# Linear attention between feed-forward products: the two heads' scores taken in turn, and the products on the tensor engine put into fewer groups

## The chip, the cores and the metric

The kernel runs on one core of a Trainium2 chip. The metric is the time of one execution on the device in microseconds. Engines are named as in the profile: PE is TensorE (matrix products), PEld its weight loads, DVE is VectorE, ACT is ScalarE, POOL is GpSimd and SP is SyncE, which issues DMAs.

## The reference

A gated linear attention over 768 steps, for 4 batches of 8 heads of width 48, is followed by two feed-forward blocks on the 384 channels of each batch.

```
f = 1.0 / (1.0 + np.exp(-f_logit))
for t in range(S):                       # S = 768, B = 4, H = 8, D = 48
    state = f[:, :, t, :, None] * state + np.einsum('bhd,bhe->bhde', k[:, :, t], v[:, :, t])
    y[:, :, t] = np.einsum('bhd,bhde->bhe', q[:, :, t], state)
# x: (B, S, 384) from y
h = gelu(x @ w_in)                       # 384 -> 1024; u, v its halves
v_n = normalised(v) * g_ln
v_s = np.einsum('ts,bsd->btd', w_sg, v_n) + b_sg[None, :, None]
x = x + (u * v_s) @ w_out
theta = x @ w_theta
y = np.einsum('ts,bsd->btd', w_tok_r, x * cos(theta)) + np.einsum('ts,bsd->btd', w_tok_i, x * sin(theta))
u = x + y
out = u + np.maximum(u @ w_ch, 0.0)
```

## The kernel before, in words

**Attention.** The sequence is cut into blocks of 128 steps. Within a block the decays are multiplied up, so that the recurrence becomes products of matrices. A *unit* (function `unit`, from L547) treats two heads (j = 0, 1) over half a sequence (hf = 0, 1), that is three blocks c of 128 steps. There are 4 batches x 2 halves x 4 pairs of heads, 32 units. Head 0 lies in partitions 0 to 47 of the tile `qkv` (in batch 0's second half of tiles named `ar`), head 1 in 64 to 111. A unit's work on PE before the change is:

- three transposes of the keys into one bank of PSUM (L567), which ACT copies to `kt` (L571);
- the scores of head 0, three products, and then, as an operation of its own, those of head 1 (L580); each has a bank, and DVE multiplies each by the causal mask into a tile `am` (L585);
- the updates of the state (L596), two for each block, with the last block left out where hf is 1; DVE and ACT make from them the chain of states `s` (L609, L619);
- three operations of outputs, one for each block: two masked products, `am` with the values (L631), and, where there is a state before the block, two state products (L635), which add to the same columns. ACT copies the bank to `y` (L639), and POOL sends it to `xst` by DMA (L647).

The products are of float32, and each stands in the trace as two instructions. So the scores of a unit are twelve instructions at L580, the masked products twelve at L631, the updates twelve or eight at L596, the state products eight (hf 0) or twelve (hf 1) at L635.

**Feed-forward blocks.** `mm3` (L666 to L668) makes one product of two split operands by three matrix products of 384 or 512 columns. Their weights are decoded by DVE and ACT (L413 to L434) from wide floats while the products run.

**Order.** The class `Plan` writes out the order of every engine's instructions ahead of time. Each operation is given a duration, on PE a number of columns too, and a virtual time at which it is wanted. A list schedule takes, at each step, the operation that can start first and, among those, the one wanted first. Buffers of a kind (`Slots`) are taken in the order in which they were asked for; attention has four banks of PSUM, `at`, and in the first half of batch 0 those of the feed-forward blocks, `mm`, too. Attention of batch 1 is spread over the first feed-forward block of batch 0, and that of batches 2 and 3 over later work. Up to a planned time of 100 us, gaps on PE are filled with products of no use (`idle`, L908), written into bank `at0` beside the columns in use. On the chip each engine follows its order and waits at semaphores.

Of the kernel before, what the change touches and what calls it, by code (L numbers as in the profile page):

```python
# [17 lines left out]
P = 128  # L18
# [70 lines left out]
class Buf:  # L89
    """A tile (or a part of one) whose readers and writers order each other."""  # L90
# [9 lines left out]
class Part:  # L100
    """A part of a tile, by its first free index."""
# [13 lines left out]
class Plan:  # L115
    """Orders the instructions of each engine: a list schedule over their estimated times."""
# [47 lines left out]
    @staticmethod  # L164
    def loads(o, table):
        """the activation tables that the operation has to load ("T": tanh, which two of them have)"""
        if o.table is None or o.table == table or (o.table == "T" and table in ("G", "S")):
            return None
        return "G" if o.table == "T" else o.table

    def schedule(self):
# [14 lines left out]
        def slot_time(o):  # L186
            t = 0.0
            for b in o.need:
                if b.held:
                    continue  # L190
                s = b.slots
                if s.order[s.next] is not b:
                    return None
                best = None
                for i in range(s.n):
                    prev = s.owner[i]
                    if prev is None:
                        u = 0.0
                    else:
                        u = 0.0  # L200
                        for a in prev.acc:
                            if a.end is None:
                                u = None
                                break
                            u = max(u, a.end + (0.0 if a.dma else lat(a.eng, o.eng)))
                    if u is not None and (best is None or u < best[0]):
                        best = (u, i)
                if best is None:
                    return None
                b.slot = best[1]  # L210
                t = max(t, best[0])
            return t

        def run(a, dur, left):
            """the tensor engine's clock: up after a tick with enough columns"""
            c, i = left / dur, int(a / TICK + 1e-9)
            while left > 1e-6:
                rate = c if ticks.get(i - 1, 0) >= 3060 else c / 2
                n = min(left, rate * ((i + 1) * TICK - a))
                ticks[i] = ticks.get(i, 0) + n  # L220
                left, a, i = left - n, a + n / rate, i + 1
            return a
# [89 lines left out]
def body(tc, ctx, att, qkv, flog, w_in, g_ln, w_sgT, b_sg, w_out, w_theta, w_rT, w_iT, w_ch, out):  # L312
# [67 lines left out]
    # ------------------------------------------------------------------ pieces  # L380
# [12 lines left out]
    def load_f32(pl, g, dst, src, on_act, vt, after=(), background=False):  # L393
        """dst: a function that gives the float32 tile; src: float32, or the bits of float64"""
# [31 lines left out]
    def load_split(pl, g, hi, lo, his, src, vt, scale=None, on_act=False, after=(), background=False):  # L426
        """hi, lo: buffers; his: a function that gives their tiles"""
        n = src.shape[-1]
        t = pl.buf(g.w32 if background else g.dt, [P, TH])
        load_f32(pl, g, (t, lambda: t.t[:, :n]), src, on_act, vt, after, background)  # L430
        if scale is not None:
            pl.op("ACT", a1(n), lambda: nc.scalar.mul(t.t[:, :n], t.t[:, :n], scale), [], [t], vt=vt)
        pl.op("ACT", a1(n), lambda: nc.scalar.copy(his()[0], t.t[:, :n]), [t], [], hi, vt=vt)  # L433
        pl.op("DVE", v1(n), lambda: nc.vector.tensor_sub(his()[1], t.t[:, :n], his()[0].bitcast(F32)), [t, *hi], [], lo, vt=vt)  # L434
# [47 lines left out]
    # --------------------------------------------------------------- attention  # L482
    def attention(pl, g, b, v0, v1_):
        """the gated linear attention of batch b, spread over the virtual times v0..v1_"""
# [10 lines left out]
    def half(pl, g, b, hf, xst, carry, vt, step):  # L495
# [3 lines left out]
        if b == 0 and hf == 1:  # L499
            # the feed-forward block's tiles are still free  # L500
# [23 lines left out]
        for p0, p1 in groups:  # L524
# [13 lines left out]
            # within a block the decays multiply up; at its first step the second operand starts it anew  # L538
# [8 lines left out]
    def unit(pl, g, b, hf, p, f, fb, seed, sb, be, bb, t, parts, xst, carry):  # L547
# [8 lines left out]
        # ks = -k / b: one Newton step on the seed of 1 / b  # L556
# [15 lines left out]
        ams = []  # L572
        for j in range(2):
            aps = bank(1 + j)
            am = pl.buf(g.am, [P, NC2, P])
            r = slice(64 * j, 64 * j + D)

            def scores(aps=aps, r=r):
                for c in cs:
                    nc.tensor.matmul(aps.t[:, c], K()[r, c], Q()[r, c], start=True, stop=True)  # L580

            pl.op("PE", 0.64, scores, r=[kb, qb], w=[aps], cols=576)
            pl.op(
                "DVE", v1(TH),
                lambda aps=aps, am=am: V.tensor_tensor(am.t, aps.t[:, :TH].rearrange("p (c t) -> p c t", c=NC2), mask3, ALU.mult),  # L585
                r=[aps], w=[am],
            )
            ams.append(am)
        ups = bank(3)
        nu = NC2 - hf  # the last block's state isn't needed  # L590

        def updates():
# [8 lines left out]
        pl.op("PE", 0.1 * nu, updates, r=[kt, vb], w=[ups], cols=192 * nu)  # L601
        state = carry.pop(p) if hf else None
# [23 lines left out]
        yps = bank(4)  # L626
        for c in range(NC2):

            def outputs(c=c, s=states[c]):
                for j in range(2):  # L630
                    nc.tensor.matmul(yps.t[HP * j : HP * j + HP, cs[c]], VT(c, j, HP), ams[j].t[:, c], start=True, stop=s is None)  # L631
                if s is not None:
                    for j in range(2):
                        r = slice(HP * j, HP * j + D)
                        nc.tensor.matmul(yps.t[r, cs[c]], s.t[r], Q()[r, cs[c]], start=False, stop=True)  # L635

            pl.op("PE", 0.45, outputs, r=[vb, qb, *ams] + ([states[c]] if states[c] else []), w=[yps], cols=540 if states[c] else 270)
# [14 lines left out]
    # ---------------------------------------------------------------------- MoE  # L652
    def moe(pl, g, xst, get, wmid, out_b, pace, first=False):
        """the two blocks of a batch; their before(): what the last block left over, to run in the first gap"""
# [3 lines left out]
        def mm3(ps, a, bs, start, stop, n):  # L658
            """one product of two split operands; a, bs: ((hi buffer, lo buffer), tiles)"""
# [241 lines left out]
    # -------------------------------------------------------------------- order  # L901
# [3 lines left out]
    def idle(n):  # L905
        """products of no use, which keep the tensor engine's clock up until those of use come"""
        for _ in range(n):
            nc.tensor.matmul(g.at.tiles[0][:, TH:], ident, ident, start=True, stop=True)  # L908

    pl.idle = idle  # L910
    with tc.manual_schedule():
# [20 lines left out]
        # the second blocks of the first two batches come late: their weights are decoded meanwhile  # L932
# [24 lines left out]
    # decays that float32's range doesn't carry through a block: the recurrence step by step  # L957
# [141 lines left out]
```

## Time and profile before

| what | value |
|---|---|
| median of 3 timed runs | 691.79 us |
| lowest and highest | 690.66 and 695.57 us |
| span of the profiled execution (its own time; nothing is recorded around it) | 697.4 us |
| PE, DVE, ACT busy | 97%, 69%, 61% of the span |

The span is that of one profiled execution, from its first instruction to its last. PE's busy time counts each instruction from its start to its modelled end, so instructions that overlap are shown together as one row with a count in the timeline. [...]

### The profile page before, as it was taken

How to read it: one execution, taken by the hardware profiler on the slowest of the kernel's cores; microseconds unless marked ns; L12 is line 12 of the kernel's file. 1: busy time of each engine (PE TensorE's matmuls, PEld its weight loads, DVE VectorE, ACT ScalarE, POOL GpSimd, SP SyncE). 2: the span in 40 equal slices, each digit the busy share in tenths (PEclk: the TensorE clock that was granted, in tenths of full speed). 3: DMA queues.
4: the chain of work that ended last, by engine and by line, in shares of the span. 5: the costliest groups of instructions: out<-in, count | busy, mean ns of one | idle time of the engine just before them, and what ended most of it. 6: DMA issues, size and time to landing. Idle time of an engine off the chain costs nothing.

```text
span 697.4 us, 12027 instructions
## 1 busy us (share of the span) xinstructions
PE 678.8 (97%) x4353; PEld 595.2 (85%) x4353; DVE 483.0 (69%) x1040; ACT 428.7 (61%) x905; POOL 93.7 (13%) x163
## 2 busy tenths in 40 slices
PE   7998999999999999999999999999999999998996
PEld 7765677977889989998898788889888889998995
DVE  5769986986999988755965666657754454567533
ACT  6568987955886678544973469535753455347520
POOL 2221233133131010003201211110010000000000
PEclk9556699999999999999999999999999999999999
DMA  8734356558356623348344551322143341111422
GB/s 324 264 105 137 107 176 203 190 171 284 126 159 189 220 66 135 124 123 260 109 143 147 155 175 41 98 63 75 32 155 102 94 153 35 35 50 35 162 74 73
DMA packets 42613, 93.55 MB, mean 134 GB/s; under 512 B 6064, under 2 KB 28208, under 8 KB 41520
## 3 DMA queue, kind: packets, MB, share of 16 engines
q1 hardware_dynamic: 33840, 63.00, 28.3%
q0 software_dynamic: 8704, 29.70, 13.0%
q8 instruction: 36, 0.59, 0.4%
q14 instruction: 33, 0.27, 0.1%
HBM read 76.15 MB, written 11.80 MB: 126 GB/s over the span
## 4 chain that ended last, share of the span: by engine, by line
PE 84%; DVE 6%; ACT 3%; DMA 2%; issue 2%; POOL 1%; SPq 0%; DVEq 0%; ACTq 0%; POOLq 0%
PE mm L666 22%; PE mm L668 20%; PE mm L667 20%; PE at L580 6%; PE at L631 4%; PE at L635 4%; PE at L596 2%; PE at L567 2%; PE mm L762 1%; DMA raw<-in_w_iT 1%; PE mm L580 1%; DMA f<-in_flog 1%; DMA dt<-in_w_sgT 1%; PE at L908 1%; DVE tmp L726 1%
## 5 line engine op out<-in xcount | busy, mean ns | idle before, releaser
L666 PE MATMUL mm<-st,ar 128*128 128x384 f32 x480 | 166.6, 347 | 1.9 <-ACT u L708 1.4
L667 PE MATMUL mm<-st,ar 128*128 128x384 f32 x480 | 161.3, 336 | 0.4 <-DVE st L434 0.4
L668 PE MATMUL mm<-st,ar 128*128 128x384 f32 x480 | 161.1, 336 | 0.0
L434 DVE TENSOR_TENSOR st<-dt,st 128x384 fp32r<-128x384 f32 x144 | 77.7, 553 | 72.3 <-ACT st L433 71.8
L433 ACT CAST st<-dt 128x384 fp32r<-128x384 f32 x144 | 72.7, 511 | 87.1 <-PE mm L668 54.6
L666 PEld LDWEIGHTS mm<-st,ar 128*128 128x128 f32 x480 | 90.4, 188 | 9.5 <-issue 5.1
L667 PEld LDWEIGHTS mm<-st,ar 128*128 128x128 f32 x480 | 90.5, 189 | 0.9 <-DVE st L434 0.9
L668 PEld LDWEIGHTS mm<-st,ar 128*128 128x128 f32 x480 | 90.4, 188 | 0.0
L685 ACT CAST x<-xst 128x384 fp32r<-128x384 f32 x72 | 36.1, 510 | 42.0 <-DVE xst L690 24.5
L647 POOL DMA_DIRECT2D xst<-y x80 | 40.5, 511 | 141.6 <-ACT y L639 91.5
L585 DVE TENSOR_TENSOR am<-at,mask 128x384 f32<-128x384 f32 x60 | 31.6, 550 | 22.2 <-PE at L580 14.1
L675 ACT CAST ar<-tmp 128x384 fp32r<-128x384 f32 x80 | 38.0, 511 | 8.2 <-DVE tmp L731 7.3
L686 DVE TENSOR_TENSOR x<-xst,x 128x384 fp32r<-128x384 f32 x72 | 38.6, 552 | 5.7 <-ACT x L685 5.4
L676 DVE TENSOR_TENSOR ar<-tmp,ar 128x384 fp32r<-128x384 f32 x80 | 41.0, 550 | 2.2 <-ACT ar L675 1.8
L690 DVE TENSOR_TENSOR xst<-xst,mm 128x384 f32<-128x384 f32 x48 | 26.0, 552 | 21.8 <-PE mm L668 21.6
L580 PE MATMUL at<-qkv 48*128 48x128 f32 x312 | 40.4, 298 | 0.0
L580 PEld LDWEIGHTS at<-qkv 48*128 48x128 f32 x312 | 33.4, 195 | 6.8 <-issue 5.6
L666 PE MATMUL mm<-ar,wout 128*128 128x384 f32 x96 | 33.9, 353 | 1.6 <-DVE tmp L778 1.6
L631 PE MATMUL at<-am,qkv 128*64 128x128 f32 x312 | 34.9, 306 | 0.0
L666 PE MATMUL mm<-x,win 128*128 128x384 f32 x96 | 33.9, 353 | 0.0
L518 POOL DMA_DIRECT2D qkv<-in_qkv x24 | 13.3, 554 | 147.6 <-PE at L635 132.7
L667 PE MATMUL mm<-ar,wout 128*128 128x384 f32 x96 | 32.9, 343 | 0.0
(156 smaller groups left out, 1478.9 us busy)
## 6 DMA issues: line engine op xcount, KB each, us to landing
dt<-scratch SPq DMA_DIRECT2D x96, 192.0 KB, 2.4
qkv<-in_qkv POOLq DMA_DIRECT2D x24, 536.0 KB, 4.7
dt<-in_w_sgT SPq DMA_DIRECT2D x48, 192.0 KB, 2.7
wmid<-scratch SPq DMA_DIRECT2D x6, 1152.0 KB, 5.8
raw<-in_w_rT SPq DMA_DIRECT2D x12, 384.0 KB, 4.1
raw<-in_w_iT SPq DMA_DIRECT2D x12, 384.0 KB, 3.3
f<-in_flog POOLq DMA_DIRECT2D x6, 768.0 KB, 4.9
scratch<-wt POOLq DMA_DIRECT2D x24, 192.0 KB, 3.1
```

The lines of the kernel that those rows point to most:

```text
L433: pl.op("ACT", a1(n), lambda: nc.scalar.copy(his()[0], t.t[:, :n]), [t], [], hi, vt=vt)
L434: pl.op("DVE", v1(n), lambda: nc.vector.tensor_sub(his()[1], t.t[:, :n], his()[0].bitcast(F32)), [t, *hi], [], lo, vt=vt)
L580: nc.tensor.matmul(aps.t[:, c], K()[r, c], Q()[r, c], start=True, stop=True)
L631: nc.tensor.matmul(yps.t[HP * j : HP * j + HP, cs[c]], VT(c, j, HP), ams[j].t[:, c], start=True, stop=s is None)
L647: lambda r0=r0, n=n, kc=kc, o=64 * j + off: q[YQ].dma_start(xst.t[r0 : r0 + n, kc], y.t[o : o + n]),
L666: nc.tensor.matmul(o, h0, h1, start=start, stop=False)
L667: nc.tensor.matmul(o, h0, l1, start=False, stop=False)
L668: nc.tensor.matmul(o, l0, h1, start=False, stop=stop)
L675: pl.op("ACT", a1(n), lambda: nc.scalar.copy(tiles()[0], src.t[:, :n]), [src], [hi])
L676: pl.op("DVE", v1(n), lambda: V.tensor_sub(tiles()[1], src.t[:, :n], tiles()[0].bitcast(F32)), [src, hi], [lo])
L685: pl.op("ACT", a1(TH), lambda: nc.scalar.copy(X[hf][:, 0, k], T()), [src], [hi])
L686: pl.op("DVE", v1(TH), lambda: V.tensor_sub(X[hf][:, 1, k], T(), X[hf][:, 0, k].bitcast(F32)), [src, hi], [lo])
```

## The change

- The scores of the two heads become one operation. Its instructions go block by block, head 0 and head 1 in turn. It takes two banks at once.
- The updates and all masked products of a unit become one operation, `products`. It waits for `kt` and both `am` tiles, and takes the banks of the updates and of the outputs at once.
- The state products of a unit become one operation, `carried`, which waits for all states it needs.
- In the bank of the outputs, each head's sum is opened by its first masked product (`start` only at c = 0) and stays open until its last state product.
- The planner learns to give one operation two buffers of a kind (`slot_time`). The products of no use go to a bank without an open sum (`started`).
- The durations and columns that the planner is told change with it.
- Comments are removed.

```diff
         def slot_time(o):
-            t = 0.0
+            t, taken = 0.0, {}
             for b in o.need:
...
-                if s.order[s.next] is not b:
+                mine = taken.setdefault(id(s), [])
+                at = s.next + len(mine)
+                if at >= len(s.order) or s.order[at] is not b:
                     return None
...
                 b.slot = best[1]
+                mine.append(best[1])
...
-        ams = []
+        aps = [bank(1 + j) for j in range(2)]
+        ams = [pl.buf(g.am, [P, NC2, P]) for _ in range(2)]
+        rows = [slice(HP * j, HP * j + D) for j in range(2)]
+
+        def scores():
+            for c in cs:
+                for j in range(2):
+                    nc.tensor.matmul(aps[j].t[:, c], K()[rows[j], c], Q()[rows[j], c], start=True, stop=True)
+
+        pl.op("PE", 0.85, scores, r=[kb, qb], w=aps, cols=1152)
         for j in range(2):
-            aps = bank(1 + j)
-            am = pl.buf(g.am, [P, NC2, P])
-            r = slice(64 * j, 64 * j + D)
-
-            def scores(aps=aps, r=r):
-                for c in cs:
-                    nc.tensor.matmul(aps.t[:, c], K()[r, c], Q()[r, c], start=True, stop=True)
-
-            pl.op("PE", 0.64, scores, r=[kb, qb], w=[aps], cols=576)
...
-        ups = bank(3)
-        nu = NC2 - hf  # the last block's state isn't needed
-
-        def updates():
+        ups, yps = bank(3), bank(4)
+        nu = NC2 - hf
+        state = carry.pop(p) if hf else None
+
+        def products():
+            started.append(yps.t)
             for c in range(nu):
                 for j in range(2):
...
-        pl.op("PE", 0.1 * nu, updates, r=[kt, vb], w=[ups], cols=192 * nu)
-        state = carry.pop(p) if hf else None
+            for c in range(NC2):
+                for j in range(2):
+                    nc.tensor.matmul(yps.t[HP * j : HP * j + HP, cs[c]], VT(c, j, HP), ams[j].t[:, c], start=c == 0, stop=False)
+
+        pl.op("PE", 0.12 * nu + 0.87, products, r=[kt, vb, *ams], w=[ups, yps], cols=192 * nu + 810)
...
-        yps = bank(4)
-        for c in range(NC2):
-
-            def outputs(c=c, s=states[c]):
+        late = [c for c in range(NC2) if states[c] is not None]
+
+        def carried():
+            started.pop(next(i for i, t in enumerate(started) if t is yps.t))
+            for c in late:
                 for j in range(2):
-                    nc.tensor.matmul(yps.t[HP * j : HP * j + HP, cs[c]], VT(c, j, HP), ams[j].t[:, c], start=True, stop=s is None)
-                if s is not None:
-                    for j in range(2):
-                        r = slice(HP * j, HP * j + D)
-                        nc.tensor.matmul(yps.t[r, cs[c]], s.t[r], Q()[r, cs[c]], start=False, stop=True)
-
-            pl.op("PE", 0.45, outputs, r=[vb, qb, *ams] + ([states[c]] if states[c] else []), w=[yps], cols=540 if states[c] else 270)
+                    nc.tensor.matmul(yps.t[rows[j], cs[c]], states[c].t[rows[j]], Q()[rows[j], cs[c]], start=False, stop=c == late[-1])
+
+        pl.op("PE", 0.22 * len(late) + 0.2, carried, r=[qb, *(states[c] for c in late)], w=[yps], cols=270 * len(late))
...
         for _ in range(n):
-            nc.tensor.matmul(g.at.tiles[0][:, TH:], ident, ident, start=True, stop=True)
+            t = next(t for t in g.at.tiles if not any(t is x for x in started))
+            nc.tensor.matmul(t[:, TH:], ident, ident, start=True, stop=True)
```

## Rows read from the trace of the kernel before

**Rows 1.** The page: busy time of each engine; the group of the masks on DVE.

```profile
PE 678.8 (97%) x4353; PEld 595.2 (85%) x4353; DVE 483.0 (69%) x1040; ACT 428.7 (61%) x905; POOL 93.7 (13%) x163
...
L585 DVE TENSOR_TENSOR am<-at,mask 128x384 f32<-128x384 f32 x60 | 31.6, 550 | 22.2 <-PE at L580 14.1
```

**Rows 2.** Busy us by stretch: window, length, engines (x instructions), clock, DMA.

```profile
20.00:52.00 32.00, 32.00 (x194) 22.04 (x191) 21.08 (x49) 18.65 (x46) 7.51 (x13) 0.50 0.50 167
52.00:82.50 30.50, 27.94 (x184) 17.73 (x182) 28.82 (x74) 27.23 (x60) 7.13 (x14) 0.65 0.39 116
82.50:169.20 86.70, 85.60 (x625) 66.43 (x623) 71.76 (x167) 64.14 (x144) 26.07 (x44) 0.98 0.63 203
169.20:244.20 75.00, 73.50 (x402) 70.31 (x403) 69.26 (x149) 58.62 (x124) 12.65 (x17) 1.00 0.54 174
244.20:553.40 309.20, 308.77 (x2086) 272.45 (x2084) 203.39 (x423) 181.44 (x373) 33.80 (x59) 1.00 0.37 117
```

**Rows 3.** Waits of PE, 82.5 to 553.4 us: total, times, longest; the two largest.

```profile
PE mm L666 <- ACT u L708: 1.4, 1, 1.4
PE at L635 <- ACT s L619: 1.1, 2, 0.7
```

**Rows 4.** Timeline of PE, a spread unit of hf 0: start, duration, line, tiles, count.

```profile
464.50 1.26 PE L580 MATMUL at<-qkv 48*128 48x128 f32 x12
465.69 0.45 PE L666 MATMUL mm<-st,ar 128*128 128x384 f32 x1
...
466.94 0.56 PE L596 MATMUL at<-qkv,kt 128*64 128x48 f32 x12
467.42 0.45 PE L666 MATMUL mm<-st,ar 128*128 128x384 f32 x1
467.71 0.34 PE L667 MATMUL mm<-st,ar 128*128 128x384 f32 x1
467.88 0.34 PE L668 MATMUL mm<-st,ar 128*128 128x384 f32 x1
468.15 0.44 PE L631 MATMUL at<-am,qkv 128*64 128x128 f32 x4
468.52 0.45 PE L666 MATMUL mm<-st,ar 128*128 128x384 f32 x1
```

**Rows 5.** Timeline of PE, two blocks' masked products in a row.

```profile
453.24 0.66 PE L631 MATMUL at<-am,qkv 128*64 128x128 f32 x8
453.82 0.42 PE L635 MATMUL at<-qkv,s 48*48 48x128 f32 x4
454.18 0.44 PE L666 MATMUL mm<-x,win 128*128 128x384 f32 x1
```

**Rows 6.** Timeline of PE, one head's scores alone.

```profile
429.19 0.93 PE L580 MATMUL at<-qkv 48*128 48x128 f32 x6
430.06 0.44 PE L666 MATMUL mm<-st,ar 128*128 128x384 f32 x1
```

**Rows 7.** Timeline of PE, the last unit.

```profile
547.55 0.44 PE L596 MATMUL at<-qkv,kt 128*64 128x48 f32 x8
547.82 0.40 PE L631 MATMUL at<-am,qkv 128*64 128x128 f32 x4
548.15 0.42 PE L635 MATMUL at<-qkv,s 48*48 48x128 f32 x4
...
552.76 0.44 PE L631 MATMUL at<-am,qkv 128*64 128x128 f32 x4
```

**Rows 8.** Timeline of PE, updates followed by masked products.

```profile
89.99 0.56 PE L596 MATMUL at<-qkv,kt 128*64 128x48 f32 x12
90.38 0.40 PE L631 MATMUL at<-am,qkv 128*64 128x128 f32 x4
```

**Rows 9.** Timeline of PE in batch 0's first half, at the lower clock.

```profile
24.27 1.65 PE L580 MATMUL mm<-qkv 48*128 48x128 f32 x6
25.85 0.69 PE L631 MATMUL at<-am,qkv 128*64 128x128 f32 x4
26.47 0.67 PE L635 MATMUL at<-qkv,s 48*48 48x128 f32 x4
```

More of the change, by code (lines that the diff above doesn't have):

```diff
@@ L195, in slot_time @@
                 for i in range(s.n):
+                    if i in mine:
+                        continue
                     prev = s.owner[i]
[L197 to L200, printed above, removed]
+                    u = 0.0
+                    if prev is not None:
                         for a in prev.acc:
@@ L480, in stream @@
         return w
+    started = []
     def attention(pl, g, b, v0, v1_):
@@ L571, in unit @@
         pl.op("ACT", a1(TH), lambda: nc.scalar.mul(kt.t, kps.t[:, :TH], -1.0), r=[kps], w=[kt])
-        ams = []
-        for j in range(2):
-            aps = bank(1 + j)
-            am = pl.buf(g.am, [P, NC2, P])
-            r = slice(64 * j, 64 * j + D)
-            def scores(aps=aps, r=r):
-                for c in cs:
-                    nc.tensor.matmul(aps.t[:, c], K()[r, c], Q()[r, c], start=True, stop=True)
-            pl.op("PE", 0.64, scores, r=[kb, qb], w=[aps], cols=576)
+        aps = [bank(1 + j) for j in range(2)]
[6 more added lines that the diff above has]
+        pl.op("PE", 0.85, scores, r=[kb, qb], w=aps, cols=1152)
+        for j in range(2):
             pl.op(
                 "DVE", v1(TH),
-                lambda aps=aps, am=am: V.tensor_tensor(am.t, aps.t[:, :TH].rearrange("p (c t) -> p c t", c=NC2), mask3, ALU.mult),
-                r=[aps], w=[am],
-            )
-            ams.append(am)
-        ups = bank(3)
+                lambda j=j: V.tensor_tensor(ams[j].t, aps[j].t[:, :TH].rearrange("p (c t) -> p c t", c=NC2), mask3, ALU.mult),
+                r=[aps[j]], w=[ams[j]],
+            )
+        ups, yps = bank(3), bank(4)
         nu = NC2 - hf
-        def updates():
+        state = carry.pop(p) if hf else None
+        def products():
+            started.append(yps.t)
             for c in range(nu):
```

## The prediction

> **What bounds the kernel now.** I read the page's busy shares first: TensorE (PE) is busy for 97% of the span, VectorE (DVE) for 69%, ScalarE less [rows 1]. PE's share counts pipelined ends, so it had to be confirmed by stage. [...] The waits of PE from 82.5 to 553.4 confirm it: the two longest are 1.4 and 1.1 us in 471 [rows 3]. So from 82.5 us on a microsecond of PE's instruction stream is a microsecond of the end, as long as no other engine is full. Two stretches have another one nearly full: DVE is at 28.8 of 30.5 us (94%) from 52 to 82.5 and at 69.3 of 75.0 us (92%) from 169.2 to 244.2, and it is at 83% between them [rows 2]. The last attention work on PE is at 553 us; what follows is not touched.
>
> PE's stream I read from the timeline, by starts: a block costs the time from its start to the start of the next row. Durations overlap and would count double.
>
> **What the change does to PE's stream, in units.** A unit is one pair of heads over half a sequence; there are 32: 8 of batch 0, before 82.5 us, and 24 after it. In a unit that is spread among the feed-forward products [rows 4] the scores of both heads take 1.19 us (464.50 to 465.69), the updates 0.48, a block of masked products alone 0.37. Between two such blocks three feed-forward products take 0.73 us, with steps of 0.29, 0.17 and 0.27: the middle one is the undisturbed step, so each excursion to attention costs 0.73 - 3 x 0.174 = 0.2 us beyond its own block. A block of state products takes 0.36 (453.82 to 454.18) [rows 5]. Eight masked products in a row take 0.58 (453.24 to 453.82) where four take 0.37 [rows 4, 5], so two further pairs cost 0.21, that is 0.107 a pair: the two heads of a pair run side by side there, because the code alternates them.
>
> *Scores.* Six instructions, one head, take 0.87 us with the way in and out [rows 6]; the twelve of two heads take 1.19 [rows 4]. The second head overlaps already, but late: it adds 0.32. Alternated from the first instruction it should add about nothing, as for the masked products. So a unit's scores go from 1.19 to 0.87, and where the planner had parted the two heads, from 2 x 0.87 to 0.87. The bounds are a second head that adds nothing (0.87) and one that runs serially: six further steps of (1.19 - 0.87)/3 = 0.11 us, so 1.53. I take the first, by the masked products.
>
> [...]
>
> *Updates and masked products.* In the trace an update block that runs straight into masked products takes 0.39 (twelve instructions) or 0.27 (eight), and the four masked products behind it 0.33 instead of 0.37 [rows 7, 8]: these two kinds follow each other without a gap. The new group has twelve masked products, so 0.33 + 4 x 0.107 = 0.76; with the updates 1.15 in a first half (hf 0) and 1.03 in a second (hf 1).
>
> *State products.* They come in one block: 0.36 + 2 x 0.107 = 0.57 (two blocks of the sequence, hf 0) and 0.36 + 4 x 0.107 = 0.79 (three, hf 1). No row shows more than four of them in a row; if each further pair cost as much as half of a block of two (0.18), these would be 0.72 and 1.08. I take 0.107, by the masked products, which are as wide.
>
> *Sum for a spread unit.* A pair of blocks, masked and state products, is 0.37 + 0.36 = 0.73. hf 0 before: 1.19 + 0.48 + 0.37 + 2 x 0.73 + four excursions beside the one with the transposes, 0.8, makes 4.29; after: 0.87 + 1.15 + 0.57 + 0.4 = 2.99; it saves 1.30. hf 1 before: 1.19 + 0.37 (eight updates alone: 0.27 and the 0.1 by which twelve alone exceed 0.39) + 3 x 0.73 + 0.8 = 4.55; after: 0.87 + 1.03 + 0.79 + 0.4 = 3.09; it saves 1.46. With 12 of each: 33.1 us. Not every unit is spread: the timeline from 82.5 to 553.4 has 72 entries into such blocks (the first at 89.99, the last at 552.76 [rows 7, 8]) where 96 would be full spread, so 24 x 0.2 = 4.8 us less is to be won; and in 7 units the heads' scores are parted, as in [rows 6], which adds 7 x (1.74 - 1.19) = 3.9. That leaves 32.2 us, **1.34 us a unit**.
>
> *What is added or moved elsewhere.* DVE's and ScalarE's instructions are the same in number and size, and so are the DMAs. The planner's costs and column counts change, and with them its whole order; it then runs nearer to the blocks' true lengths, so I cost this at nothing, with 2 us either way. New are three waits: the scores need two free banks at once, the updates are queued behind both masks' being planned, and the masked products stand in PE's own queue in front of whatever was planned behind them. Feed-forward products cover them after 82.5 us, since the planner can put them between. Without this cover a unit would wait for the tail of its scores and two masks of 0.55 us [rows 1].
>
> **Where the saving lands.** From 244.2 to 553.4 there are 16 units and DVE is at 66% [rows 2]: all of 16 x 1.34 = 21.4 us reaches the end. From 82.5 to 169.2 there are 8 units, 10.7 us; what is late next is DVE, whose decoding of weights has to be done all the same. At the 92% that it reaches in the stretch behind it, its 71.8 us need 77.7, so 9.0 us of the 86.7 can go [rows 2]. I take 9.
>
> [...] Alternated scores would save 1.58 in each of batch 0's first-half units, whose heads stand apart, and about 0.66 (the 0.32 at half clock) in the others; the masked products save 3 x 0.62 - (0.62 + 4 x 0.21) = 0.4. Together 4 x 2.0 + 4 x 1.1 = 12 us of PE. But this work only runs faster into the stretch in which DVE is at 94%. I take 0 of it; the bounds are 0 and 12.
>
> The forecast is 21.4 + 9.0 = 30.4 us saved. The profiled execution's span is 697.4 us, 5.6 above the median of the timed runs and 1.8 above their highest; the blocks are at full clock in both stretches that pay, so I take the saving off the median: 691.8 - 30.4 = **661 us**.
>
> **Rivals.** *DVE holds everything ahead of 244 us*: the 9 us don't come either, 691.8 - 21.4 = 670. For it: 92 to 94% in two of three stretches; against it: the 83% between. *Everything pays, batch 0 too*: 32.2 + 12 = 44 saved, 648. Against it: 170 us of DVE work in the 192 us from 52 to 244.2; at 94% it allows some 12 us in all. *The alternated scores don't run side by side*: a unit's scores take 1.53, so it loses 0.34 instead of saving 0.32; 24 x 0.66 = 16 us less, 677. Against it: 1.19 < 1.53 in [rows 4, 6]. *Slower: the merged group stalls PE.* It stands in PE's queue until both masks are there, and nothing behind it can pass. PE would stand from the scores' end for their drain (about 0.3), two masks (1.1) and the wait for DVE's queue, and then again for the chain of states, before the state products: 2.6 us a unit by estimate, if the planner had nothing to put between. 24 x (2.6 - 1.34) = 30, so 722; it decides from 1.34 + 6.9/24 = 1.6 us a unit. Against it: feed-forward work is always there after 82.5, and PE waits 2.5 us there now [rows 3]. *The new order costs what the blocks save* (a mistimed stream of weights, or attention that ends too late for its batch): 690.
>
> **How the numbers follow.** Chances: the forecast 0.57, DVE holds the early part 0.20, everything pays 0.09, no concurrency 0.05, order eats it 0.05, slower 0.04. The range reaches from nearly everything paid to the rival without concurrency: 650 to 678. Less than about 1% (7 us) can't be told from no change with this kernel; the first four cases are all beyond that: faster 0.91, same 0.05, slower 0.04.
>
> **What would show it.** In the changed profile: score blocks of twelve that take 0.87; no block of four masked products alone; blocks of updates and masked products of about 1.15 and 1.03; at most three excursions a unit; the last state product at about 522 us instead of 553; DVE above 90% up to about 160 us; PE waiting for masks less than 5 us in all. The forecast is wrong if PE waits for masks or states in the rows of the merged group, if DVE's share before 244 us stays as it is while PE shows gaps, or if further state products cost 0.18 a pair (4 us).

## The result and the profile after

The changed kernel takes 668.1 us (median; 667.8 to 671.7) against 692.3 us: a ratio of 0.967 [0.963, 0.971], 24.2 us less. Forecast were 661 us and a saving of 30.4.

Line numbers of the changed kernel: scores 585, updates 604, masked products 611, state products 643, feed-forward products 674 to 676, theta's transposes 770, masks 591, products of no use 917. Its page begins:

```profile
span 666.4 us, 12236 instructions
...
PE 636.4 (95%) x4457; PEld 584.9 (88%) x4457; DVE 479.9 (72%) x1040; ACT 430.9 (65%) x909; POOL 91.8 (14%) x163
```

Against [rows 1] PE has lost 42 us of busy time, and its share has *fallen*, to 95%: a part of what it no longer does has become waiting.

The timeline of PE in the changed kernel, two spread units, first one of hf 1 and then one of hf 0, answers to [rows 4 to 8]:

```profile
497.75 0.94 PE L585 MATMUL at<-qkv 48*128 48x128 f32 x12
498.62 0.44 PE L674 MATMUL mm<-st,ar 128*128 128x384 f32 x1
...
500.91 0.44 PE L604 MATMUL at<-qkv,kt 128*64 128x48 f32 x8
501.18 0.84 PE L611 MATMUL at<-am,qkv 128*64 128x128 f32 x12
501.95 0.44 PE L674 MATMUL mm<-st,ar 128*128 128x384 f32 x1
...
503.71 0.86 PE L643 MATMUL at<-qkv,s 48*48 48x128 f32 x12
504.50 0.45 PE L674 MATMUL mm<-st,ar 128*128 128x384 f32 x1
```

```profile
440.96 0.56 PE L604 MATMUL at<-qkv,kt 128*64 128x48 f32 x12
441.35 0.84 PE L611 MATMUL at<-am,qkv 128*64 128x128 f32 x12
442.12 0.45 PE L674 MATMUL mm<-st,ar 128*128 128x384 f32 x1
...
443.91 0.64 PE L643 MATMUL at<-qkv,s 48*48 48x128 f32 x8
444.48 0.44 PE L674 MATMUL mm<-st,ar 128*128 128x384 f32 x1
```

Read by starts, the scores take 0.87 us, updates and masked products 0.27 + 0.77 and 0.39 + 0.77, the state products 0.79 and 0.57. The forecast had 0.87, 1.03 and 1.15, 0.79 and 0.57. Every block has the length that was put down for it.

The profile that the prediction was read from had an unusually long span. The first run below took another one of the same kernel; it is the one that the rest is compared with. The table has starts on PE, in us from the span's start, read from the timelines: the last state products of batches 0 and 1, the first transposes of theta (the second feed-forward block of batch 0), the last state product of all, and the span.

| kernel | batch 0 | batch 1 | theta | last | span |
|---|---|---|---|---|---|
| before, shown profile | 82.3 | 168.9 | 244.3 | 553.3 | 697.4 |
| before, second profile | 79.1 | 163.4 | 238.7 | 547.9 | 691.8 |
| changed | 70.4 | 153.6 | 227.2 | 520.0 | 666.4 |

Of the 25.4 us between the last two rows 8.7 come in batch 0's attention, 1.1 in batch 1's, 1.7 up to theta, and 13.9 behind it. In the table of stretches, the second profile of before, cut at theta, reads:

```profile
16.00:238.70 222.70, 219.52 (x1423) 176.47 (x1422) 194.28 (x444) 171.86 (x376) 53.49 (x87) 0.89 0.58 184
...
238.70:691.80 453.10, 443.42 (x2833) 403.02 (x2831) 279.94 (x579) 246.70 (x512) 36.55 (x63) 0.99 0.34 104
```

and the changed kernel, cut at its own theta:

```profile
16.00:227.20 211.20, 198.19 (x1531) 173.83 (x1532) 193.85 (x448) 175.08 (x379) 53.24 (x89) 0.98 0.60 198
...
227.20:666.40 439.20, 424.54 (x2833) 397.56 (x2831) 277.99 (x576) 245.31 (x514) 34.70 (x61) 0.99 0.34 106
```

Columns are the length, then the busy time of PE, PEld, DVE, ACT and POOL, then PE's granted clock, the DMA engines' share and GB/s. Ahead of theta PE is busy for 21.3 us less, although 104 more instructions of no use are among it and in part because the granted clock is higher (0.98 for 0.89; one head's scores take 1.58 us at 0.50 [rows 9] and 0.87 at 1.00 [rows 6]), and stands 9.8 us more (13.0 against 3.2), so 11.5 come through. DVE's work is the same, 194 us, and its share rises from 87 to 92%. Behind theta, at the same clock, PE has 18.9 us less to do and stands 5.0 more (14.7 against 9.7), so 13.9 come through. Together PE is busy for 40 us less and stands for 15 us more.

The two stretches are not equally firm. Behind theta the two profiles of the kernel before agree to 0.1 us (697.4 - 244.3 and 691.8 - 238.7 are both 453.1); ahead of it they differ by 5.6 us, the whole difference of their spans.

### The profile page after: what moved, and what is told of

Its sections match the earlier page's. It is cut to its first block, busy times and chain, and to the rows that moved or that the text cites. A ratio compares the mean times of both kernels' runs of the same rounds, so it can differ in the third digit from the quotient of the medians.

```text
span 666.4 us, 12236 instructions
## 1 busy us (share of the span) xinstructions
PE 636.4 (95%) x4457; PEld 584.9 (88%) x4457; DVE 479.9 (72%) x1040; ACT 430.9 (65%) x909; POOL 91.8 (14%) x163
## 4 chain that ended last, share of the span: by engine, by line
PE 62%; DVE 11%; ACT 9%; DMA 7%; issue 7%; POOL 1%; SPq 1%; DVEq 0%; POOLq 0%; ACTq 0%
PE mm L674 19%; PE mm L675 18%; PE mm L676 18%; DMA ar<-in_qkv 3%; DMA f<-in_flog 2%; DMA qkv<-in_qkv 2%; PE at L643 2%; PE at L585 2%; PE at L611 1%; PE at L917 1%; ACT L303 1%; DVE tmp L786 1%; DVE tmp L734 1%; DMA wmid<-scratch 1%; DVE ar L684 1%
## 5 line engine op out<-in xcount | busy, mean ns | idle before, releaser
L917 PE MATMUL at<-ident 128*128 128x128 f32 x216 | 31.3, 307 | 7.3 <-DVE am L591 3.0
L917 PEld LDWEIGHTS at<-ident 128*128 128x128 f32 x216 | 29.4, 219 | 8.8 <-DVE am L591 3.4
L674 PE MATMUL mm<-ar,wout 128*128 128x384 f32 x96 | 33.7, 351 | 2.6 <-DVE tmp L786 2.3
L675 PE MATMUL mm<-ar,wout 128*128 128x384 f32 x96 | 32.8, 342 | 0.0
L676 PE MATMUL mm<-ar,wout 128*128 128x384 f32 x96 | 32.7, 341 | 0.0
```

The source lines that it names most:

```text
L674: nc.tensor.matmul(o, h0, h1, start=start, stop=False)
L675: nc.tensor.matmul(o, h0, l1, start=False, stop=False)
L676: nc.tensor.matmul(o, l0, h1, start=False, stop=stop)
L917: nc.tensor.matmul(t[:, TH:], ident, ident, start=True, stop=True)
```

## The experiments

Each kernel was timed beside the kernel before on the same chip. Its time has to be read against 668 us; the kernel before took 691.1 to 692.7 us in all of these series, so times of different series can be compared. Its stretches have to be read against the table above. They come from one profiled execution of each kernel, which took up to 4 us more or less than the median, so ahead of theta a few microseconds between two kernels mean little.

**The kernel before again.** No edit.

> The kernel before, once more, with the span and the granted clock of each execution. The profile of the kernel before had a span of 697.4 us at a mean clock of 0.954, 7 us above the median time less what lies around a span (1.7 us in the changed kernel). Theory A: that profile caught an unusually long execution, with the lower clock early on; most executions have spans of 689 to 692 at a higher mean clock (0.96 or more), and a new profile shows a clock above 0.50 in part of 20 to 52 us. Theory B: the profiled execution is like the others and only the profile makes it longer; then spans are 689 to 692 at the same clock, 0.954, and the new profile shows 0.50 from 20 to 52 us again.

Measured: 691.6 us, ratio 1.001 [0.998, 1.004]; the new profile has a span of 691.8 at a mean clock of 0.959 (0.954 in the first). Theory A holds in the main: the execution shown before was a long one (the ten spans here are 685.7 to 694.3 us), and the new profile has a clock of 0.99 from 16 to 27 us, where the first has 0.63. But from 27 to 52 us the clock is 0.50 in both, although PE is busy all the time: the low clock there is seen in both profiles of this kernel.

**Head after head in the one scores operation.**

```diff
-            for c in cs:
-                for j in range(2):
+            for j in range(2):
+                for c in cs:
                     nc.tensor.matmul(aps[j].t[:, c], ...)
```

> The changed kernel with one difference: inside the one scores operation the six instructions of head 0 come first and then those of head 1, as before. The planner sees no difference, so the order of everything else stays. Theory: score blocks go from 0.87 back to 1.19 us, and after 70 us, where TensorE sets the end, 24 x 0.32 = 7.7 us come back: 675 to 677 us. Rival 1: the scores' blocks are hidden behind waits for masks and for the copied keys, then 668 to 671. Rival 2: the turns matter only ahead of 70 us at the lower clock, then the time after 70 us stays within 2 us.

Measured: 673.5 us, 0.975 [0.969, 0.980], 5.4 above the changed kernel. A score block in its timeline:

```profile
504.26 1.26 PE L585 MATMUL at<-qkv 48*128 48x128 f32 x12
505.45 0.44 PE L674 MATMUL mm<-st,ar 128*128 128x384 f32 x1
```

It takes 1.19 us again. Theta starts at 228.6, 1.4 later, and from there to the end it takes 4.3 us more, where 16 x 0.32 = 5.1 were expected. The order of all operations is the same in both kernels, so this is the price of the turns alone: 4.3 of the 5.1 us behind theta. The 1.4 of 2.6 ahead of it are less than two profiles of one kernel differ there.

**The groups without the joined scores.**

```diff
-        def scores():
+        def scores(j):
...
-        pl.op("PE", 0.85, scores, r=[kb, qb], w=aps, cols=1152)
+        for j in range(2):
+            pl.op("PE", 0.64, lambda j=j: scores(j), r=[kb, qb], w=[aps[j]], cols=576)
```

> The changed kernel with the scores as two operations again, one per head (planned at 0.64 each), and with the merged groups of updates and masked products and of state products as changed. Theory: 7.7 us as with the turns off, and the 7 or so units whose heads the planner parts add 0.55 each: 676 to 681 us. Rival: taking two banks at once is what costs waits in the changed kernel, then parting the scores gives some of it back: 670 to 674.

Measured: 690.2 us, 0.999 [0.996, 1.002]: no gain is left, far from both expectations. Batch 0's attention ends at 74.0, 5 us earlier than before, but theta starts at 238.0, where it did before. Behind theta it saves 3.7 us instead of 13.9. The largest wait there:

```profile
PE mm L674 <- DMA wmid<-scratch: 5.1, 1, 5.1
```

Between the second block of batch 0 and that of batch 1 the weights `wmid`, which have one buffer, are loaded anew. In the second profile of before, attention fills PE for 7 us in that place (313.97 to 321.15), and no such wait is listed. Here it ran out early. In the changed kernel the same place has 5.5 us of attention (300.92 to 306.4) and a wait of 1.6.

**The joined scores without the groups.**

```diff
-        pl.op("PE", 0.12 * nu + 0.87, products, r=[kt, vb, *ams], w=[ups, yps], ...)
+        pl.op("PE", 0.1 * nu, updates, r=[kt, vb], w=[ups], ...)
...
-        pl.op("PE", 0.22 * len(late) + 0.2, carried, ...)
+        for c in range(NC2):   # masked and state products of one block, as before
+            pl.op("PE", 0.45, outputs, ...)
```

> The changed kernel with the scores in turn, but with the updates as an operation of their own and one operation of masked and state products per block, with a closed sum each, as before. Theory: the groups are worth about 0.85 us a unit after 70 us (1.34 less 0.32 for the turns less 0.16 for parted heads), 24 x 0.85 = 20, a part of it hidden behind VectorE ahead of 230 us: 683 to 689 us. Rival: the gain of the changed kernel is mostly the early stretch at the higher clock, which the groups don't make: 672 to 678.

Measured: 674.6 us, 0.975 [0.971, 0.979]: better than expected. Batch 0's attention ends at 66.0, theta starts at 230.0. So 8.7 us come ahead of theta and 7.1 behind it, of the changed kernel's 11.5 and 13.9. The two parts don't add: alone the groups gave nothing, and with the joined scores they give 6.5 us. In each of these kernels the planner makes another order, so neither number is the price of the blocks alone.

**Products of no use in batch 0 of the kernel before.**

```diff
+    def warm(b, fn):        # batch 0: fn(), then two products of no use
...
-        pl.op("PE", 0.64, scores, r=[kb, qb], w=[aps], cols=576)
+        pl.op("PE", 0.64, warm(b, scores), r=[kb, qb], w=[aps], cols=576)
```

(and so at the transposes, updates and outputs)

> The kernel before, with two products of no use (128 columns, float32) behind each attention operation of batch 0 on TensorE, 112 more in all; nothing else changes, the planner doesn't know of them. In the kernel before, TensorE is never idle from 27 to 52 us but is granted 0.50; in the changed kernel and with the turns alone it is granted 1.00 for most of that time, and batch 0's attention ends at 66 to 70 us instead of 79. Theory: the changed kernel's early gain is the clock's, and what raises it is that the tensor engine's stream then holds full-width products between the narrow ones. Then these additional products raise the clock to 1.00 over most of 27 to 70 us, and batch 0's attention ends 5 to 10 us earlier although TensorE has more to do: 682 to 687 us. Rival: the clock follows from the two heads being side by side in the scores; then it stays at 0.50, and 112 products of 0.21 us only add work: 700 us or more.

Measured: 706.8 us, 1.023 [1.015, 1.031]. Stretches from 27 to 38 and 38 to 52 us, here and, below it, in the changed kernel with the products of no use left out after 15 us, the next experiment:

```profile
27.00:38.00 11.00, 11.00 (x102) 8.73 (x101) 4.36 (x10) 4.25 (x8) 1.58 (x3) 1.00 0.32 89
38.00:52.00 14.00, 13.98 (x117) 10.56 (x117) 6.76 (x18) 7.02 (x16) 2.64 (x5) 1.00 0.35 109
```

```profile
27.00:38.00 11.00, 8.44 (x80) 5.98 (x77) 10.93 (x30) 10.27 (x26) 3.31 (x7) 0.66 0.67 204
38.00:52.00 14.00, 11.23 (x62) 7.54 (x63) 12.46 (x29) 13.01 (x28) 3.63 (x7) 0.50 0.65 205
```

The theory was right on the clock, the column after POOL's: it is 1.00 where the kernel before had 0.50. It was wrong on the time: the 112 products are 224 instructions, 24 us by the 0.21 us a product that the rival put down, and batch 0's attention ends at 92.6 us instead of 79.1. The higher clock didn't pay for the work that was added.

**No products of no use after 15 us.** The changed kernel with

```diff
-WARM_TO = 100.0
+WARM_TO = 15.0
```

> The changed kernel, with the planner's products of no use after a planned time of 15 us left out (about 120 of the 216). Theory of the clock by full-width products: it falls back to 0.50 for much of 20 to 52 us, batch 0's attention ends at about 74 us as in the run with the groups only, and the time is 671 to 676 us. Rival: the score turns keep the clock up by themselves, and the products of no use only delay attention: 666 to 668.

Measured: 669.0 us, 0.969 [0.961, 0.977], not to be told from the changed kernel. As the theory had it, the clock fell to 0.50 and 0.66, and batch 0's attention ended 2.4 us later, at 72.8. But theta starts at 221.7, 5.5 earlier, and the rest takes 444.1 us instead of 439.2. The time came out below the theory's range and above the rival's. So the 24 us don't need the higher clock of the early stretch.

**Decoding spread further.** The changed kernel with

```diff
-BG_TO = 80.0
+BG_TO = 115.0
```

> The changed kernel, with the decoding of the token weights, which fills VectorE behind the first batches, spread to 115% of their two first blocks instead of 80%. From 70 to 227 us of the changed kernel VectorE is at 90 to 93% and TensorE waits 6.5 us between 70 and 154. Theory: VectorE holds this stretch, so moving some 8 us of its work behind 230 us shortens the stretch by 3 to 6 us: 662 to 666. Rival: the waits there come from the order alone, since VectorE has its idle time in other places; then no change within 2 us, or a loss where weights come late for the second block.

Measured: 673.6 us, 0.975 [0.967, 0.983]; theta at 228.2, and behind it 3.9 us more. From 70 to 228 us DVE's work fell by 2.6 us only (142.2 for 144.9), not by 8. It tells nothing about DVE ahead of theta, and the rival's loss behind it came.

**State products one block at a time.**

```diff
-        def carried():
-            for c in late:
...
+        for c in late:
+            pl.op("PE", 0.42, carried, r=[qb, states[c]], w=[yps], cols=270)   # two products
```

> The changed kernel, with the state products as one operation per block again (two or three a unit) instead of one; the sum stays open, and the group of updates and masked products stays. Theory: each additional operation costs one more excursion, 0.2 us, and loses the 0.14 by which two further pairs in a row (0.22) are cheaper than a block of two alone (0.36): 12 units x 1 and 12 x 2 operations after 70 us, up to 36 x 0.34 = 12 us if the planner spreads them all: 674 to 680. Rival: the planner puts them side by side, as it is the same data that they wait for: 668 to 671.

Measured: 679.8 us, 0.983 [0.975, 0.991]. In its timeline a unit's state products stand apart, with feed-forward products between:

```profile
517.05 0.42 PE L645 MATMUL at<-qkv,s 48*48 48x128 f32 x4
...
518.12 0.42 PE L645 MATMUL at<-qkv,s 48*48 48x128 f32 x4
...
519.20 0.42 PE L645 MATMUL at<-qkv,s 48*48 48x128 f32 x4
```

Behind theta it takes 443.3 us, 4.1 more, half of the 24 x 0.34 = 8.2 that full spread would cost there. Ahead of theta it loses 9.8 us, most of it to waits: theta starts at 237.0 although batch 0's attention ends 5.7 us earlier. The total fell into the expected range, but not by the expected sum.

**Planned durations set to the measured ones**, in the changed kernel and in the kernel before.

```diff
-        pl.op("PE", 0.85, scores, ...)      # changed kernel; also products and carried, by under 0.09
+        pl.op("PE", 0.87, scores, ...)
```

> The changed kernel; only the three durations that the planner is told are nudged by at most 0.09 us to what its trace shows (scores 0.87, products 1.16 and 1.04, state products 0.57 and 0.79). Theory: the order is worth some microseconds by itself, because TensorE no longer has work to put over every wait; the blocks keep their lengths, and the time moves by 2 to 6 us either way, by waits. Rival: the planner's small errors of cost don't matter, as the prediction took it: 666 to 670 us.

```diff
-            pl.op("PE", 0.64, scores, ...)  # before; updates 0.1 * nu to 0.117 * nu + 0.13
+            pl.op("PE", 0.87, scores, ...)
-            pl.op("PE", 0.45, outputs, ...)
+            pl.op("PE", 0.72 if states[c] else 0.37, outputs, ...)
```

> The kernel before; only the planned durations of its attention operations on TensorE are set to what its trace shows (scores 0.87, updates 0.48 and 0.36, an output operation 0.72, the first of a sequence 0.37). Theory: in the kernel before TensorE's stream has no gaps after 82 us that a better order could close, so the time stays within 4 us of 691 and blocks on TensorE keep their lengths. Rival: part of the changed kernel's gain is that its planner is told nearer durations; then this gives 4 to 10 us of the 24: 681 to 687.

Measured: 673.3 us, 0.974 [0.970, 0.978], 5.2 above the changed kernel, and 714.8, 1.032 [1.026, 1.038], 23 above the kernel before. The first is as the theory had it; the second is outside both expectations. With the same blocks, batch 0's attention ends at 62.5 in the first, 8 us earlier, and theta starts at 234.1, 7 us later. In the second, batch 0's attention ends at 94.1, 15 us later. PE's longest waits there are for masks and copied keys:

```profile
PE at L631 <- DVE am L585: 7.8, 4, 4.0
PE at L596 <- ACT kt L571: 5.7, 3, 2.0
```

So the planner's numbers alone, a part of this change, can move the time by about as much as the whole change does, and in neither of these two runs did numbers nearer to the trace make a better order.

**The scan in halves.** In the changed kernel, DVE's scan of the decays stands ahead of theta's products, and PE waits for these:

```profile
243.77 3.35 DVE L541 TENSOR_TENSOR_SCAN f<-f,seed 128x1536 f32<-128x1536 f32 x1
...
247.04 0.99 DVE L786 TENSOR_TENSOR tmp<-mm,tmp 128x384 f32<-128x384 f32 x2
...
248.18 0.52 PE L770 MATMUL mm<-ident,xst 128*128 128x128 f32 x3 [1.12 <-DVE tmp L786]
```

```diff
-        groups = (GROUPS0, GROUPS1)[hf] if b == 0 else [(0, NP)]
+        groups = (GROUPS0, GROUPS1)[hf] if b == 0 else [(0, 2), (2, NP)]
```

> The changed kernel; for batches 1 to 3 the work on the decays goes in two groups of two pairs of heads instead of one of four, so that the longest VectorE instruction, the scan, takes 1.7 us instead of 3.35. In the changed kernel that scan starts at 243.8 us ahead of the products of theta's sines, and TensorE waits 1.1 us for these at 247. Theory: the waits that were covered by attention's work before come from such long instructions; halving them takes the wait at 247 away and shortens others: 662 to 666 us, with under 3 us of listed waits between 227 and 520 us instead of 4.5. Rival: the waits come from the whole chain (loads, decoding, the order), and other ones take its place; more instructions and table loads: 667 to 674.

Measured: 668.8 us, 0.968 [0.962, 0.974]: no change. The listed waits from theta to the last attention are 3.9 us instead of 4.5: the one for the sines fell from 1.1 to 0.4, others came. The rival is nearer.

**A part of DVE's work to GpSimd.**

```diff
-        pl.op("DVE", v1(TH), lambda: V.tensor_mul(Q(), Q(), F()), r=[fb], w=[qb])
+        if b < 2:
+            pl.op("POOL", 0.95, lambda: nc.gpsimd.tensor_tensor(Q(), Q(), F(), ALU.mult), r=[fb], w=[qb])
+        else: ...   # as before
```

> The changed kernel; in the units of batches 0 and 1 the product of the queries with the decays (128x384, 0.55 us on VectorE, one a unit) goes to GpSimd, 16 products, 8.8 us of VectorE's work. In ten kernels VectorE has 191 to 197 us of work between 16 us and the first transposes of theta, at 222 to 238 us (92% of the stretch in the changed kernel, whose theta starts at 227). Theory: ahead of that point VectorE and no longer TensorE sets the pace in the changed kernel; VectorE's work there falls to about 185 us, theta starts 5 to 10 us earlier, at 217 to 222, and the time is 659 to 664 us. Rival: the stretch is set by the order and by chains of waits, with VectorE busy only because it has 8% of slack; theta stays within 3 us of 227 and the time within 666 to 672. Second rival: GpSimd is too slow for it or slows VectorE's own instructions; then VectorE's 128x384 products take more than 0.55 us and the time is 669 or more.

Measured: 666.9 us, 0.963 [0.959, 0.966], not to be told from the changed kernel's 0.967 [0.963, 0.971]. Theta starts at 225.2, 2 us earlier, which is less than two profiles of one kernel differ there. DVE's work ahead of it did not fall: 194.9 us from 16 to 225.2. It lost 7 us of products (9.2 fell to 2.2) and got as much back in instructions that took longer, one of them 3.57 us while GpSimd's products ran (the last section has the rows). So the run could not test whether DVE sets the pace there.

## Why the prediction was right, point by point

**What bounds the kernel.** That PE's stream sets the end from 82.5 us on held for the kernel before. It did not hold for the changed one, in which PE stands 15 us more from 16 us on. Most of the 6 us between forecast and result hang on this. (The "two longest" waits of 1.4 and 1.1 us that the prediction read from [rows 3] are totals; the second is two waits, the longer of 0.7. Nothing hangs on it.)

**The blocks.** All five lengths came out to 0.01 us, the state products in a longer row too (0.107 a further pair, not 0.18). The scores run side by side: head after head costs 1.19, in turn 0.87; the serial 1.53 was seen in no run. The rival without concurrency is out.

**"All of 16 x 1.34 = 21.4 us reaches the end."** This step was mis-sized: 13.9 us came behind theta. PE had 18.9 us less to do there, and it stood 5.0 us longer, 4.1 of them up to the last attention. Why its work fell by 18.9 and not by 21.4, though every block has its length, stays open. The waits of the changed kernel from theta to the last attention, against [rows 3]:

```profile
PE mm L674 <- DMA wmid<-scratch: 1.6, 1, 1.6
PE mm L770 <- DVE tmp L786: 1.1, 1, 1.1
PE mm L674 <- DVE s L620: 0.7, 2, 0.4
PE mm L674 <- DVE tmp L786: 0.7, 1, 0.7
```

These are not the waits of the merged group on masks that the prediction named as new. They are latencies of the feed-forward blocks (a load into a single buffer, theta's sines behind a long scan); in the second profile of before a single wait of 0.4 us is listed from theta to the last attention. In the prediction's own terms: the feed-forward products cover attention, but attention also covers the feed-forward blocks, and the change shortened that cover. For `wmid` the timelines show it: 7.2 us of attention and no wait before, 5.5 us and a wait of 1.6 in the changed kernel, a wait of 5.1 with the groups only. For the other waits it is argued and not shown.

**"9.0 us ahead of 244", and "0" of batch 0.** The sum was near, 11.5 us up to theta, by luck: 8.7 came in batch 0, which was put at 0, and 2.8 from its end to theta, put at 9.0. The bound of 12 us on batch 0 is summed from the starts in [rows 9], 1.58 us for one head's scores and 0.62 for four masked products at the granted 0.50 of [rows 2]; no run shows the 12, and 8.7 came. Why batch 0 was put at 0, that its work "only runs faster into the stretch in which DVE is at 94%", overlooked that DVE had idle time from 27 to 52 us (17.6 of 25 us busy in the second profile of before), into which its own work moved forward. In the changed kernel it is full there, at 10.9 of 11.0 and 14.0 of 14.0 us. First the second profile of before, then the changed kernel:

```profile
27.00:38.00 11.00, 11.00 (x72) 6.83 (x72) 7.12 (x19) 6.81 (x15) 2.06 (x4) 0.50 0.52 152
38.00:52.00 14.00, 14.00 (x84) 10.08 (x80) 10.52 (x32) 9.77 (x28) 3.68 (x7) 0.50 0.52 152
```

```profile
27.00:38.00 11.00, 9.78 (x118) 7.52 (x115) 10.90 (x30) 10.55 (x28) 4.62 (x9) 1.00 0.67 217
38.00:52.00 14.00, 9.44 (x83) 8.38 (x83) 13.97 (x32) 11.80 (x21) 1.80 (x4) 0.88 0.55 172
```

The clock differs there too (0.50 against 1.00 and 0.88), but in the changed kernel without the products of no use, at 0.66 and 0.50, batch 0's attention still ends at 72.8, with 6.3 of the 8.7 us.

The 9.0 us were to come in the stretch of batch 1, under a cap of DVE at 92%. There 1.1 came. The same stretch in the second profile of before and in the changed kernel:

```profile
79.40:163.70 84.30, 83.94 (x625) 65.11 (x623) 71.11 (x165) 64.62 (x144) 26.20 (x44) 1.00 0.64 202
```

```profile
70.70:153.90 83.20, 76.70 (x626) 65.00 (x626) 75.25 (x179) 69.25 (x158) 26.75 (x45) 0.96 0.67 218
```

PE is busy for 7.2 us less and stands 6.5 us instead of 0.4. The largest of these waits is one of the three that the prediction named as new and took as covered, that of the scores for two free banks. Rows of PE and then of ACT:

```profile
141.34 0.48 PE L585 MATMUL at<-qkv 48*128 48x128 f32 x2
144.32 1.65 PE L585 MATMUL at<-qkv 48*128 48x128 f32 x10 [2.50 <-ACT kt L576]
```

```profile
142.40 1.48 ACT L532 ACTIVATE f<-f 128x1536 f32<-128x1536 f32 x1 [3.48 <-DMA f<-in_flog]
143.79 0.47 ACT L576 ACTIVATE kt<-at 128x384 f32<-128x384 f32 x1
```

Head 0's first product has run. Head 1's waits 2.50 us for ACT's copy to `kt`; the scores don't read `kt`, so what they wait for is the bank that this copy frees. The copy is queued behind work on the decays, and that stood 3.48 us for a load. Right behind the wait PE's granted clock is 0.50 for 6.7 us:

```profile
144.30:151.00 6.70, 6.68 (x46) 5.64 (x48) 5.82 (x14) 5.58 (x12) 2.09 (x4) 0.50 0.88 303
```

By estimate, half of these 6.7 us are lost at a clock of 0.50; with the 2.50 us of the wait that makes some 5 to 6 of the 7.9 us that are missing. That the wait brought the lower clock is not shown. Nor is the late load shown to be what holds the stretch: in the last experiment the load comes in time and no such wait is listed, and its stretch of batch 1 takes 83.4 us all the same, with 6.2 us of other waits.

The cap of DVE is neither shown nor excluded. The changed kernel has DVE at 91.8% from 16 us to theta (193.85 of 211.2), but variants in which batch 0's attention ends at 62.5 to 72.8 us start theta at 221.7 to 237.0, at 88 to 93%. Of the two attempts to take work off DVE there, one took 2.6 us off and the other none.

**"I cost this at nothing, with 2 us either way."** The 2 us had no ground in the rows, and the runs speak against them. The same blocks under durations changed by at most 0.09 us gave 5.2 us more, and in the kernel before, durations corrected from the trace gave 23 more. So the planner's order can be a term of the size of the whole change. How much of this change's 24 us it gave or took is not known: no run has the new blocks in the old order. Other orders with the same attention blocks on PE lie anywhere from 667 to 674 us in the runs here.

**The profile and the median.** The saving was taken off the median although the profile was 5.6 us above it. Taken between two usual executions the spans differ by 25.4, the times by 24.2. The 31.0 between the first profile and the changed one would have looked like a hit for the wrong reason. So the 6.2 us between forecast and result are 7.5 us too much behind theta, 2.5 too little ahead of it, and 1.2 between spans and times.

**Rivals.** Slower, by PE standing for the masks: waits for masks in the changed kernel are 0.7 us at L611 in the whole span, and 3.0 at products of no use in the first batches; it stays out. "The order costs what the blocks save" did not come for this change, but it is what happened to the groups alone (690.2), so its chance of 0.05 looks low. Of the signs, the masks came (3.7 us of waits, under 5) and the last state product (520.0 us for about 522), the latter in part because batch 0, which was put at 0, ended earlier.

What stays open: why the order with the scores joined and the groups merged keeps 24 us and that with the groups alone keeps nothing. In the latter, 3.5 us more for `wmid` and the scores' 16 x 0.32 = 5.1 us would make most of the 10.2 us that it loses behind theta; ahead of theta, 5 us won by 74 us are lost again by 238, and no single wait over 1.5 us is listed for it.

## What to carry to other kernels

Counting instruction starts in a trace gives the length of a new block to the hundredth of a microsecond; what such a block saves in the end depends on what it covered, so look for the loads and long chains that the shortened work stood over. An operation that takes two buffers at once stands for the later of them, as the scores did for 2.50 us behind one late load. Where a planner writes the order, a change of its numbers is a change of its own, to be run alone, and a few microseconds between two orders of the same work say little on the blocks in them. Take more than one profile of the kernel before where a sum is made against it.

## What the runs showed of the hardware

**Two row halves overlapped more when they were issued in turn.** Twelve score instructions, six for each head (48 rows from partition 0 and from 64), take 1.19 us head after head and 0.87 in turn; one head's six alone take 0.87 as well [rows 6]. So head after head the second head adds 0.32 us, less than its own 0.87, and in turn it adds nothing.

**A low clock under a busy engine.** PE was busy for all of 27 to 52 us in both profiles of the kernel before and was granted 0.50; in the first, 142 of its 155 instructions there are products of 48 rows or 64 columns. In the run with two products of no use, of 128 columns, behind each attention operation of batch 0, PE ran 219 instructions in these 25 us instead of the second profile's 156, was busy for 24.98 us and was granted 1.00. What of this sets the clock is not shown.

**VectorE took longer beside GpSimd's products.** In the last run a VectorE instruction of a line whose median is 0.35 us in the changed kernel took 3.57, from 104.54 on, while GpSimd worked on three products, from 104.92 to 107.88. Rows of VectorE and then of GpSimd:

```profile
104.54 3.57 DVE L423 TENSOR_SCALAR wt<-raw 128x384 int32<-128x384 int32 x1
...
104.92 2.96 POOL L566 TENSOR_TENSOR qkv<-qkv,f 128x384 f32<-128x384 f32 x3
```

By the rows VectorE's instruction started 0.38 us before the first of GpSimd's three, and it ended 0.23 us after the last. From 16 us to theta seven groups of VectorE's instructions (those of L418 and L419 on two tiles each, and of L423, L562 and L564) have a higher mean than in the changed kernel, by 23 to 258 ns an instruction. Over all their instructions that comes to about 7 us, as much as the moved products took off; that each of them took longer because of GpSimd is not shown.
